# Cluster attention and a softplus FFN on one core: the first batch prepared in pairs of heads, evictions on a choice of engines, weights paced by the scores, and filler matmuls in planned waits

## The chip, the cores and the metric

The kernel runs on one core of one Trainium2 chip. The core has five engines that work side by side, each in its own program order: TensorE (PE in the profile, its weight loads PEld), VectorE (DVE), ScalarE (ACT), GpSimd (POOL) and SyncE (SP, which here only starts transfers). The metric is the device time of one execution in microseconds. The median of three runs before the change is 906.73 us.

## What is computed

Four batches of eight heads, 768 tokens, head size 64. Each query and each key is given to the nearest of 16 centroids of its head (by cosine), and a query attends only to keys of its own cluster. What comes out is a matrix of 3072 tokens by 512, which goes through a two-layer network with a softplus between the layers.

```python
q_assign = np.argmax(np.einsum('bhsd,hcd->bhsc', q_n, c_n), axis=-1)
k_assign = np.argmax(np.einsum('bhsd,hcd->bhsc', k_n, c_n), axis=-1)
mask = q_assign[:, :, :, None] == k_assign[:, :, None, :]
scores = np.where(mask, scale * np.matmul(q, k.transpose(0, 1, 3, 2)), -1000000000.0)
attn = np.exp(scores - np.max(scores, axis=-1, keepdims=True))
attn = attn / (np.sum(attn, axis=-1, keepdims=True) + 1e-09)
x = merge_heads(np.matmul(attn, v))
...
h = x @ w_in
g = np.maximum(h, 0.0) + np.log1p(np.exp(-np.abs(h)))
return (g @ w_out).astype(np.float32)
```

## The kernel before

**Numbers in two halves.** Operands of TensorE are split into a high half of 16 bits and the rest (a cast on ScalarE, then a subtraction on GpSimd); products are sums of three matmuls of halves. The mask rides along in the same matmul: the key operand carries in 16 extra columns a large negative number for every cluster that isn't its own, the query operand carries a one for its cluster, so masked scores are driven down without a separate step.

**Passes and tiles.** A pass is one batch and half of its tokens (three blocks of 128): eight passes. In a pass each of the eight heads has three score tiles of 128 queries by 768 keys, 24 tiles in all. A tile goes through `scores` (four matmuls at L544 into one of two PSUM buffers of the tag s, a row maximum on VectorE at L560, an exponential on ScalarE at L568), then the probabilities are split (L607, L609) and turned by a transposing DMA (a flip, L618), and `attend` multiplies them with the values. In pass 0 alone the probabilities stay in 32 bits, are turned on TensorE (L585), evicted from PSUM (L591 on VectorE, L593 on ScalarE) and multiplied with the raw values (L647).

**Preparation.** `prep_k` takes the keys of two heads: cast, subtract, turn (`turn`, on TensorE for batch 0 with evictions at L380 and L382, by a flip later), similarities with the centroids (`nearest`, L394 and L395), the nearest cluster, the mask (L444), a second turn. `clusters` counts by a matmul with ones (L456) which clusters have keys at all (L461, L464). `prep_q` does the like for four heads at once; it waits for the keys of all four, since queries whose cluster has no key are treated differently. `prep_v` splits the values.

**Weights.** Both weight matrices come as 64-bit floats in 32 steps of 512 columns. `prep_weights` makes 32-bit floats of their bits with one ScalarE and three VectorE instructions (L303, L305, L309, L315), then splits them (L318, L319). The raw words lie in the room of `wo` that is filled last.

**FFN.** `ffn1` of a pass starts when all four head pairs of the pass are turned into `xT` (16 blocks of twelve matmuls, L720 to L722), `softplus` works on VectorE and ScalarE (L739 to L751, split at L762 and L763), `ffn2` makes the output (L784 to L786) with two rounds of half the inner width, and `store` scales it, adds (L800, L804) and sends it (L807).

**The order.** Nothing of the order is written out by hand. Every chain of work is a Python generator that yields operations with an engine, a duration and a way to emit them. The class `Order` keeps a clock for each engine and always emits the operation that could start first by its own durations, the smaller priority number first among equals. Waits inside it (`od.set`, `wait`, rings of buffers) exist in the plan only; on the chip each engine runs its instructions in the emitted order and waits for data alone. So a changed duration, priority or planned wait changes the order of instructions on each engine, and nothing else. Transfers are planned by one clock `od.dma` for loads and flips together. VectorE and GpSimd operations marked `shared` are planned one after the other. Loads are started from ScalarE's queue (L204), flips and stores from SP's.

Of the kernel before, what the change touches and what calls it, by code (L numbers as in the profile page):

```python
# [8 lines left out]
F16 = mybir.dt.float16  # L9
# [10 lines left out]
DDS = 1024  # L20
LAG = 4
AHEAD = 10
NPE = 8
# [4 lines left out]
class Order:  # L28
# [8 lines left out]
    def __init__(self):  # L37
        self.free = dict.fromkeys(self.LAT, 0.0)
        self.ev, self.blocked, self.active = {}, {}, []
        self.dma = 0.0  # L40
        self.shared = {"DVE": 0.0, "POOL": 0.0}
        self.rings = {}
        self.cur, self.seq = None, 0

# [6 lines left out]
    def get(self, tag, size):  # L51

        k = self.rings.get(tag, 0)
        self.rings[tag] = k + 1
        return ("wait", (tag, k - size)) if k >= size else None, (tag, k)
# [23 lines left out]

    def run(self):  # L80
        while self.active:
            best = None
            for ch in self.active:
                _, eng, ns, _, opt = ch["op"]
                start = max(ch["now"], self.free[eng])
                if opt.get("shared"):
                    start = max(start, self.shared["POOL" if eng == "DVE" else "DVE"])
                prio = ch["prio"]() if callable(ch["prio"]) else ch["prio"]
                key = (start, prio, ch["seq"])
                if best is None or key < best[0]:  # L90
                    best = key, ch
            (start, _, _), ch = best
# [3 lines left out]
            if opt.get("shared"):  # L96
# [12 lines left out]
def tile_cluster_attention__then__softplus_ffn(  # L109
# [18 lines left out]
    SH = S // 2  # L128
    QT = 3

    passes = [(b, c0) for b in range(B) for c0 in range(0, NT, QT)]
    NF = DFF // P
    SCALE = 1.0 / math.sqrt(D)
    nb = QT * P

# [54 lines left out]

    def op(eng, ns, emit, **opt):
# [10 lines left out]

    def load(dst, src, nbytes):
        return op("ACT", 60, lambda: nc.scalar.dma_start(dst, src), dma=nbytes / 290.0)  # L204
# [10 lines left out]
    def prep_centroids():  # L215
# [8 lines left out]
        yield op("DVE", 150, lambda: V.tensor_tensor(sq, cf, cf, ALU.mult), dma=0)  # L224
# [45 lines left out]
    def prep_weights(step: int):  # L270
# [32 lines left out]
        yield op("ACT", 630, lambda: nc.scalar.activation(mag, val, AF.Abs, scale=sc))  # L303
# [14 lines left out]
        yield op("ACT", 610, lambda: nc.scalar.copy(part[:, 0], val))  # L318
        yield op("POOL", 1160, lambda: nc.gpsimd.tensor_tensor(part[:, 1], val, part[:, 0], ALU.subtract), shared=True)  # L319
# [11 lines left out]
    def raw_tile(nm, n, shape):  # L331

        if n < H and nm != "q":
# [3 lines left out]
        return key, p2.tile(shape, F32, tag="raw", name=f"raw{nm}_{n}")  # L337

    raw_v = {}

    def prep_v(n: int):
# [10 lines left out]
        yield op(  # L352
            "POOL",
            1640,
            lambda: nc.gpsimd.tensor_tensor(vb[:, :, :, :D], vf, vb[:, :, :, D : 2 * D], ALU.subtract),
            shared=True,
        )
# [7 lines left out]
    def turn(dst, src, name: str, on_chip: bool):  # L365
# [4 lines left out]
        for g in range(0, dst.shape[1], NT):  # L370
            hk = yield from ring("h", 2)
            ps = ps_h.tile([P, NT, P], F16, tag="h", name=f"{name}_{g}")

            def emit(g=g, ps=ps):
                for c in range(NT):
# [3 lines left out]
            if g:  # L379
                yield op("DVE", 950, lambda g=g, ps=ps: nc.vector.tensor_copy(dst[:, g : g + NT], ps))  # L380
            else:
                yield op("ACT", 820, lambda g=g, ps=ps: nc.scalar.copy(dst[:, g : g + NT], ps))  # L382
            od.set(hk)

    def nearest(xs, heads, low: int, sfx: str):
# [3 lines left out]
        ps = ps_h.tile([P, 2 * nt, NCL], F32, tag="h", name=f"sim_{sfx}")  # L389
        sim = ps[:, :nt]  # L390
# [7 lines left out]
        mx = p2.tile([P, nt, 1], F32, tag="mx", name=f"mx_{sfx}")  # L398
# [3 lines left out]
        best = p2.tile([P, nt, 1], F32, tag="best", name=f"best_{sfx}")  # L402
        yield op("DVE", 345, lambda: nc.vector.tensor_reduce(best, sim, AX.X, ALU.max))
        return ps, sim, best.to_broadcast(shp)

    def next_n2():
        key = yield from ring("n2", 2)
        return key, N2[key[1] % 2]
# [3 lines left out]
    def prep_k(n: int):  # L412
# [5 lines left out]
        nk = yield from ring("n1", 2)  # L418
        kt = p2.tile([P, 2, 2, NT, P], F16, tag="kt", name=f"kt_{n}", bufs=NP)
        kT[n], kT[n + 1] = kt[:, :, 0], kt[:, :, 1]  # L420
        n1 = p2.tile([P, 2 * NT, P], F16, tag="n1", name=f"kn1_{n}")
        od.set(("kn", n))
        yield op("ACT", 830, lambda: nc.scalar.copy(n1[:, :, D:], kf))
        yield op(
            "POOL", 1640, lambda: nc.gpsimd.tensor_tensor(n1[:, :, :D], kf, n1[:, :, D:], ALU.subtract), shared=True
        )
        od.set(rk)
        kt0 = kt[:, 0].rearrange("p h c t -> p (h c) t")
        yield from turn(kt0, n1, f"kT0_{n}", n < NPE)
        n2k, n2 = yield from next_n2()  # L430
        yield op("ACT", 830, lambda: nc.scalar.copy(n2[:, :, :D], n1[:, :, D:]))
        od.set(nk)
        h = n % H
        yield wait("cents")
        hk = yield from ring("h", 2)
        ps, sim, best = yield from nearest(
            [kt0[:, c] for c in range(2 * NT)], [h] * NT + [h + 1] * NT, 2, f"k{n}"
        )
        eq = p2.tile([P, 2 * NT, NCL], F16, tag="eq", name=f"eq_k{n}")
        yield op("DVE", 345, lambda: nc.vector.tensor_tensor(eq, sim, best, ALU.is_equal))  # L440
        yield op(
            "DVE",
            250,
# [438 lines left out]
```

## Time and profile before

| what | value |
|---|---|
| median of three runs | 906.73 us (905.98 to 908.38) |
| the profiled execution | 904.0 us, of it 902.2 us from the first to the last instruction (span) |
| mean granted clock of TensorE | 0.973 |
| busy of TensorE | 823.7 us, 91% of the span |
| busy of VectorE, ScalarE, GpSimd | 560.8, 589.4, 523.9 us |
| moved by DMA | 136 MB, 99 MB of it by flips |

The profile shows one execution. A view by stages gives the busy time of each engine in a stretch, the clock that TensorE was granted (1.00 is full speed) and the share of the 16 DMA engines that was busy. A view of waits gives, for an engine, what ended its idle time: "PE h L720 <- DVE fg L751: 6.2, 4, 3.3" says that TensorE's matmuls at line 720 waited four times for a VectorE instruction at line 751 that reads or writes fg, 6.2 us in all and 3.3 at most. In rows of instructions "x3" stands for several of one kind in a row, and the time in brackets is the idle time just before. In rows of groups the busy time and the mean duration in ns stand behind the bar.

### The profile page before, as it was taken

The page shows a single profiled execution, that of the slowest core. Times are in us where ns is not written, and L with a number is a line of the kernel's source. Part 1 is how long each engine was busy: PE and PEld are TensorE (multiplying, and loading weights), DVE is VectorE, ACT ScalarE, POOL GpSimd, SP SyncE. Part 2 cuts the span into 40 slices and gives each one's busy share as a digit, 9 for nine tenths or more (in the row PEclk, how much of TensorE's full clock was granted, in tenths as well). Part 3 has the DMA queues.
Part 4 walks back from the last instruction along what each step waited for, and adds up shares of the span by engine and source line. Part 5 has one row for each costly group of instructions (what it writes and reads, how often), then busy time and mean ns, then how long its engine had stood idle before and what let it go on. Part 6 is the DMA issues. An engine that isn't in the chain of part 4 may idle for free.

```text
span 902.2 us, 19238 instructions
## 1 busy us (share of the span) xinstructions
PE 823.7 (91%) x7843; PEld 520.0 (58%) x7843; DVE 560.8 (62%) x1034; ACT 589.4 (65%) x904; POOL 523.9 (58%) x353
## 2 busy tenths in 40 slices
PE   2669797889679999999999999999999999999996
PEld 2558684555335666666666666666666666655542
DVE  5889787778685665675766666666665645433331
ACT  5657477886458877876767777867677676633320
POOL 5233326896548778777677676776676565512210
PEclk9979699999799999999999999999999999999998
DMA  6323439999546979999888779998867755600000
GB/s 222 95 94 120 130 128 195 199 226 237 141 123 159 202 171 202 223 203 230 157 199 179 162 149 206 207 211 182 171 155 161 133 115 138 126 9 25 12 1 35
DMA packets 393320, 136.02 MB, mean 151 GB/s; under 512 B 369680, under 2 KB 386064, under 8 KB 393232
## 3 DMA queue, kind: packets, MB, share of 16 engines
q1 hardware_dynamic: 371472, 99.15, 54.9%
q10 hardware_dynamic: 21760, 35.66, 13.0%
q8 instruction: 61, 1.00, 0.5%
q14 instruction: 27, 0.22, 0.1%
HBM read 35.68 MB, written 6.29 MB: 47 GB/s over the span
## 4 chain that ended last, share of the span: by engine, by line
PE 72%; DMA 4%; DVE 3%; POOL 3%; issue 2%; ACT 2%; POOLq 0%; DVEq 0%; ACTq 0%
PE s L544 10%; PE o L786 9%; PE o L784 9%; PE o L785 9%; PE h L720 8%; PE h L722 8%; PE h L721 8%; PE av L651 3%; PE av L653 3%; PE av L652 3%; DMA pt<-phl 3%; POOL phl L609 2%; DMA xT<-xn 1%; ACT p L568 1%; DVE negm L560 1%
## 5 line engine op out<-in xcount | busy, mean ns | idle before, releaser
L609 POOL TENSOR_TENSOR phl<-p,phl 128x768 f16<-128x768 f32 x168 | 277.2, 1666 | 90.9 <-ACT phl L607 54.2
L560 DVE TENSOR_REDUCE negm<-s 128x1 f32<-128x768 f32 x192 | 182.9, 954 | 67.5 <-PE s L544 65.2
L568 ACT ACTIVATE p<-s,negm 128x768 f32<-128x768 f32 x192 | 172.3, 898 | 72.9 <-DVE negm L560 47.7
L763 POOL TENSOR_TENSOR gh<-fg,gh 128x768 f16<-128x768 f32 x64 | 105.7, 1652 | 134.5 <-ACT gh L762 134.0
L720 PE MATMUL h<-xT,wi 128*128 128x384 f16 x512 | 167.9, 328 | 14.6 <-DVE fg L751 6.2
L722 PE MATMUL h<-xT,wi 128*128 128x384 f16 x512 | 168.1, 328 | 0.0
L721 PE MATMUL h<-xT,wi 128*128 128x384 f16 x512 | 168.0, 328 | 0.0
L544 PE MATMUL s<-kt,qt 128*128 128x384 f16 x768 | 158.5, 330 | 10.2 <-ACT p L568 10.0
L784 PE MATMUL o<-wo,gh 128*128 128x512 f16 x384 | 146.3, 381 | 4.9 <-ACT gh L762 3.3
L786 PE MATMUL o<-wo,gh 128*128 128x512 f16 x384 | 146.5, 382 | 1.4 <-POOL gh L763 1.4
L785 PE MATMUL o<-wo,gh 128*128 128x512 f16 x384 | 146.4, 381 | 0.1
L741 ACT ACTIVATE fa<-fa 128x384 f32<-128x384 f32 x128 | 66.6, 521 | 114.8 <-DVE fa L739 114.1
L607 ACT CAST phl<-p 128x768 f16<-128x768 f32 x168 | 134.1, 827 | 7.1 <-DMA pt<-phl 5.5
L739 DVE TENSOR_SCALAR fa<-h 128x384 int32<-128x384 int32 x128 | 71.1, 556 | 104.0 <-PE h L722 102.8
L651 PE MATMUL av<-vb,pt 128*128 128x65 f16 x1008 | 108.7, 192 | 1.9 <-DMA pt<-phl 1.8
L652 PE MATMUL av<-vb,pt 128*128 128x64 f16 x1008 | 108.7, 192 | 0.0
L653 PE MATMUL av<-vb,pt 128*128 128x65 f16 x1008 | 108.4, 194 | 0.0
L544 PEld LDWEIGHTS <-qt 128*128 128x128 f16 x768 | 72.7, 99 | 58.5 <-issue 15.1
L751 DVE SCALAR_TENSOR_TENSOR fg<-h,fa 128x384 f32<-128x384 f32 x128 | 70.6, 552 | 57.1 <-ACT fa L742 54.5
L651 PEld LDWEIGHTS <-pt 128*128 128x128 f16 x1008 | 93.6, 98 | 15.7 <-DMA pt<-phl 3.4
L652 PEld LDWEIGHTS <-pt 128*128 128x128 f16 x1008 | 92.9, 97 | 11.8
L653 PEld LDWEIGHTS <-pt 128*128 128x128 f16 x1008 | 93.1, 97 | 0.0
(114 smaller groups left out, 1193.6 us busy)
## 6 DMA issues: line engine op xcount, KB each, us to landing
wo<-in_moe_w_in_dram ACTq DMA_DIRECT2D x16, 512.0 KB, 3.6
wo<-in_moe_w_out_dram ACTq DMA_DIRECT2D x14, 512.0 KB, 3.9
rawk<-in_k_dram ACTq DMA_DIRECT2D x16, 384.0 KB, 4.8
rawv<-in_v_dram ACTq DMA_DIRECT2D x16, 384.0 KB, 4.8
rawq<-in_q_dram ACTq DMA_DIRECT2D x16, 384.0 KB, 4.2
out_dram<-ot SPq DMA_DIRECT2D x24, 256.0 KB, 2.5
pt<-phl SPq DMA_TRANSPOSE x84, 5.5
wraw<-in_moe_w_out_dram ACTq DMA_DIRECT2D x2, 512.0 KB, 3.7
```

What stands on the lines that cost most here:

```text
L544: nc.tensor.matmul(st[:, j, :SH], qt[:, s, i], kt[:, s, NT // 2 * j : NT // 2 * (j + 1)], start=(s == 0), stop=(s == 1),)
L560: yield op("DVE", 950, lambda: nc.vector.tensor_reduce(negm, st[:, :, :SH], AX.XY, ALU.max, negate=True))
L609: "POOL", 1640, lambda: nc.gpsimd.tensor_tensor(phl[:, u, 1], p32, phl[:, u, 0], ALU.subtract), shared=True
L651: nc.tensor.matmul(av, pt[:, 0, c], vb[:, c, D : 2 * D + 1], start=(c == 0), stop=False)
L652: nc.tensor.matmul(av[:, :D], pt[:, 0, c], vb[:, c, :D], start=False, stop=False)
L653: nc.tensor.matmul(av, pt[:, 1, c], vb[:, c, D : 2 * D + 1], start=False, stop=(c == NT - 1))
L720: nc.tensor.matmul(hp, w[0], x[0], start=(c == 0), stop=False)
L721: nc.tensor.matmul(hp, w[0], x[1], start=False, stop=False)
L722: nc.tensor.matmul(hp, w[1], x[0], start=False, stop=(c == NP - 1))
L784: nc.tensor.matmul(po, g[0], wo[:, f, 0, 0], start=(f == f0), stop=False)
L785: nc.tensor.matmul(po, g[0], wo[:, f, 0, 1], start=False, stop=False)
L786: nc.tensor.matmul(po, g[1], wo[:, f, 0, 0], start=False, stop=(f == f0 + NF // 2 - 1))
```

## The change

**Preparation of the first batch.** In pass 0 the queries of a head pair are prepared by themselves (`first_q`, then `prep_q` for two heads); they wait for the living clusters of their own pair, and only where these are used. For batch 0 the keys' two operands share one tile, so the copy at L431 is dropped there, and that tile comes from buffers that are free at that time (tags xT and phl); its zero columns are cleared by four memsets on GpSimd. PSUM buffers for this preparation come from any of the tags h, o and s that has room (`bank`); those of the probabilities in pass 0 from h or o.

**Masks and clusters.** The mask is computed from the 32-bit similarities in PSUM, no longer from a 16-bit copy in SBUF; the count runs on the mask, and the living clusters come from a comparison of its sums in PSUM (two VectorE instructions as before). This holds for all batches.

**A choice of engines.** Evictions of on-chip turns and the high halves of weights go to ScalarE or VectorE, subtractions to GpSimd or VectorE, whichever the planner finds free first; a subtraction goes to VectorE only where GpSimd would end more than 2 us later, the weights' cast likewise.

**Weights.** A step of `prep_weights` waits in the plan, ahead of its first ScalarE instruction, until a given score tile has been emitted (`WGATE + step * WPACE`, step 31 at tile 43), and has a priority that goes with it.

**Planner.** Loads and flips are planned by two clocks, each at half speed while the other is at work; a flip is planned at 148 ns a block and 1200 ns behind it instead of 180 and 1500. `warm` puts matmuls of 120 columns into waits of TensorE that the plan shows to be over 600 ns, for 65% of their length. The products of pass 0 share a PSUM bank with the columns that these matmuls write.

**Others.** The last head pair of pass 0 is turned into `xT` on TensorE instead of by a flip. `ffn2` waits in the plan for its first input before it takes its PSUM buffer. Some planned durations are set anew.

The constants FIRST = 3 and MIX leave the passes and the 32-bit tiles of pass 0 as they were.

```diff
+WGATE = 0
+WPACE = 1.4
+WDUE = 4
...
+WARM = 120
+WARM_FROM = 600
+WARM_SHARE = 0.65
+SLACK = 0
+BIAS = 2000
+WBIAS = 2000
+MIX = "ffffffffffff"
+EARLY = "hos"
+PTB = "ho"
...
             self.active.remove(ch)
-            _, eng, ns, emit, opt = ch["op"]
+            if eng == "PE" and self.warm:
+                self.warm(start - self.free["PE"])
...
-            if "dma" in opt:
-                self.dma = max(self.dma, start + 900) + opt["dma"]
-                end = max(self.dma, start + ns) + 1500
+            if "flip" in opt:
+                self.flips = max(self.flips, start + 900) + opt["flip"] * (2.0 if self.loads > start else 1.0)
+                end = max(self.flips, start + ns) + 1200
+            if "load" in opt:
+                self.loads = max(self.loads, start + 1200) + opt["load"] * (2.0 if self.flips > start else 1.0)
+                end = self.loads + 1200
...
+    mbank = ps_m.tile([P, 512], F32, name="mbank")
+    idle = mbank[:, 512 - WARM :]
+
+    def warm(gap):
+        if gap > WARM_FROM:
+            for _ in range(int(gap * WARM_SHARE / 52)):
+                nc.tensor.matmul(idle, eye, ones[:, :WARM], start=True, stop=True)
...
+    def evict(dst, src, size):
+        return op(
+            ("ACT", "DVE"),
+            (180 + size * 0.8, 160 + size * 1.04),
+            (lambda: nc.scalar.copy(dst, src), lambda: nc.vector.tensor_copy(dst, src)),
+        )
+
+    def sub(dst, a, b, size):
+        return op(
+            ("POOL", "DVE"),
+            (150 + size * 1.95, 120 + size * 1.08),
+            [lambda e=e: e.tensor_tensor(dst, a, b, ALU.subtract) for e in (nc.gpsimd, nc.vector)],
+            shared=True,
+            bias=BIAS,
+        )
+
+    banks = {"s": (ps_s, 2), "h": (ps_h, 2), "o": (ps_o, 1)}
+
+    def bank(tags, shape, dtype, name):
+        tag = next((t for t in tags if od.room(t, banks[t][1])), tags[0])
+        key = yield from ring(tag, banks[tag][1])
+        return key, banks[tag][0].tile(shape, dtype, tag=tag, name=name)
...
-            "SP", 150 * blocks + 100, lambda: nc.sync.dma_start_transpose(out=dst, in_=src), dma=180.0 * blocks
+            "SP", 150 * blocks + 100, lambda: nc.sync.dma_start_transpose(out=dst, in_=src), flip=148.0 * blocks
...
-        yield op("ACT", 630, lambda: nc.scalar.activation(mag, val, AF.Abs, scale=sc))
+        gate = int(WGATE + step * WPACE)
+        if gate >= 0:
+            yield wait("sc", gate)
+        yield op("ACT", 660, lambda: nc.scalar.activation(mag, val, AF.Abs, scale=sc))
...
+        if n < H:
+            tag = "xT" if n < H // 2 else "phl"
+            keys = [(yield from ring(tag, 2))]
+            n12 = p2.tile([P, 2 * NT, P + D], F16, tag=tag, name=f"kn12_{n}")
+            n1, n2 = n12[:, :, :P], n12[:, :, D:]
+            nc.gpsimd.memset(n2[:, :, D + NCL :], 0.0)
...
-        yield op("DVE", 345, lambda: nc.vector.tensor_tensor(eq, sim, best, ALU.is_equal))
-        yield op(
-            "DVE",
-            250,
-            lambda: nc.vector.tensor_scalar(n2[:, :, D : D + NCL], eq, 1.0, MASK, ALU.subtract, ALU.mult),
-            shared=True,
-        )
+        yield op("DVE", 345, lambda: nc.vector.tensor_tensor(sim, sim, best, ALU.is_equal))
+        mask = n2[:, :, D : D + NCL]
+        yield op("DVE", 345, lambda: nc.vector.tensor_scalar(mask, sim, 1.0, MASK, ALU.subtract, ALU.mult))
...
+    def first_q(n: int):
+        qkey[n, 0] = yield from ring("qt", 2)
+        nt = passes[0][2]
+        rk, qf = yield from load_q(n, 0)
+        qt = p2.tile([P, 2, 4, nt, P], F16, tag="qt", name=f"qt_{n}_0")
+        for u in range(4):
+            qT[n + u, 0] = qt[:, :, u]
+        for u in (0, 2):
+            od.spawn(prep_q(n + u, 0, 2, qf[:, u : u + 2], qt[:, :, u : u + 2], rk if u else None), od.cur["prio"] + u * nt)
...
-        yield wait("q", n - n % 4, pi)
+        yield wait("q", n - n % (4 if pi else 2), pi)
...
-        yield flip(
-            xT[pi][:, pr].rearrange("p s c t -> p (s c) t"), t_.rearrange("p s c d -> p (s c d)"), 2 * QT
+        yield from turn(
+            xT[pi][:, pr].rearrange("p s c t -> p (s c) t"),
+            t_.rearrange("p s c d -> p (s c) d"),
+            f"xT_{pr}_{pi}",
+            pi == 0 and pr == NP - 1,
         )
...
-        od.spawn(prep_weights(step), begin - 12 + step * 0.6)
+        od.spawn(prep_weights(step), WGATE + WDUE + step * WPACE)
```

More of the change, by code (lines that the diff above doesn't have):

```diff
@@ L78, in pump, with start @@
         self.cur = outer
+    def start(self, ch, eng):
+        t = max(ch["now"], self.free[eng])
+        if ch["op"][4].get("shared") and eng in self.shared:
+            t = max(t, self.shared["POOL" if eng == "DVE" else "DVE"])
+        return t
     def run(self):
         while self.active:
-            best = None
+            ready = []
             for ch in self.active:
[L84 to L87, printed above, removed]
+                eng, ns = ch["op"][1:3]
+                if isinstance(eng, tuple):
+                    _, ns, eng = min((self.start(ch, e) + n + (e != eng[0]) * ch["op"][4].get("bias", 0), n, e) for e, n in zip(eng, ns))
@@ L88, in run @@
                 prio = ch["prio"]() if callable(ch["prio"]) else ch["prio"]
[L89 to L92, printed above, removed]
-            self.active.remove(ch)
-            _, eng, ns, emit, opt = ch["op"]
+                ready.append((self.start(ch, eng), prio, ch["seq"], eng, ns, ch))
+            soon = min(ready, key=lambda r: r[:3])
+            start, _, _, eng, ns, ch = min(
+                (r for r in ready if r[3] == soon[3] and r[0] <= soon[0] + SLACK), key=lambda r: (r[1], r[0], r[2])
+            )
@@ L337, in raw_tile, with next_n2 @@
         return key, p2.tile(shape, F32, tag="raw", name=f"raw{nm}_{n}")
+    def next_n2():
+        key = yield from ring("n2", 2)
+        return key, N2[key[2] % 2]
     raw_v = {}
@@ L447, in prep_k @@
-        od.spawn(clusters(n, ps, eq, hk), od.cur["prio"])
-        yield from turn(kt[:, 1].rearrange("p h c t -> p (h c) t"), n2, f"kT1_{n}", n < NPE)
-        od.set(n2k)
+        hk, ps = yield from bank(EARLY if n < H else "h", [P, 4 * NT, NCL], F32, f"sim_k{n}")
+        sim, best = yield from nearest(
+            ps[:, : 2 * NT], [kt0[:, c] for c in range(2 * NT)], [h] * NT + [h + 1] * NT, 2, f"k{n}"
+        )
+        yield op("DVE", 345, lambda: nc.vector.tensor_tensor(sim, sim, best, ALU.is_equal))
@@ L450, in prep_k, with clusters @@
+        mask = n2[:, :, D : D + NCL]
+        yield op("DVE", 345, lambda: nc.vector.tensor_scalar(mask, sim, 1.0, MASK, ALU.subtract, ALU.mult))
+        od.spawn(clusters(n, ps, mask, hk), od.cur["prio"])
+        yield from turn(kt[:, 1].rearrange("p h c t -> p (h c) t"), n2, f"kT1_{n}", n < H)
+        for key in keys:
+            od.set(key)
         od.set(("k", n))
-    def clusters(n, ps, eq, hk):
+    def clusters(n, ps, mask, hk):
         h = n % H
         cnt = ps[:, 2 * NT :]
-        yield op("PE", 100, lambda: nc.tensor.matmul(cnt, ones, eq, start=True, stop=True))
+        yield op("PE", 100, lambda: nc.tensor.matmul(cnt, ones, mask, start=True, stop=True))
@@ L630, in attend @@
         n, pi, i = tiles[t]
+        nt = passes[pi][2]
         h = n % H
```

289 lines of the change are left out of this document (154 added, 135 removed).

## The prediction

> **What bounds the kernel now.** I read the time by stages first, then TensorE's waits in each stage, then the order of time in the first one. The first view is the busy time of each engine by stage: the length, then busy us of PE, PEld, DVE, ACT and POOL, then the granted clock and the share of the DMA engines. The stages are the preparation before the first scores, the 24 score tiles of pass 0, the change to the mixed flow, the mixed flow itself, and the tail.
>
> ```profile
> core 0: us, PE busy (x) PEld busy (x) DVE busy (x) ACT busy (x) POOL busy (x), PEclk, DMA share, GB/s
> 0.00:54.00 54.00, 23.02 (x295) 19.48 (x296) 38.63 (x114) 28.60 (x41) 22.64 (x23) 0.92 0.46 152
> 54.00:139.00 85.00, 76.01 (x570) 64.23 (x568) 74.96 (x120) 57.26 (x113) 25.88 (x22) 0.89 0.42 121
> 139.00:300.00 161.00, 132.05 (x1329) 79.79 (x1327) 113.06 (x198) 113.63 (x173) 113.28 (x76) 0.96 0.85 185
> 300.00:860.00 560.00, 559.89 (x5508) 341.71 (x5507) 325.37 (x589) 382.23 (x566) 357.21 (x231) 1.00 0.75 155
> 860.00:902.20 42.20, 32.77 (x150) 14.81 (x148) 8.81 (x15) 7.72 (x13) 4.91 (x3) 0.92 0.05 19
> ```
>
> From 300 to 860 us TensorE is busy for 559.89 of 560 us at full clock. Its matmuls there are the same after the change, so nothing can be won in that stretch. All that can be won lies in the idle time of TensorE elsewhere: 31.0 us in the first stage, 9.0 in the second, 29.0 in the third, 9.4 in the tail, and in the granted clock, which is below 1.00 in those four alone. VectorE is busy for 75.0 of 85 us in the second stage, nearly as full as TensorE.
>
> The second view is TensorE's waits over the whole run, longest first in total (total us, times, longest).
>
> ```profile
> PE centsT L250 <- DVE cb L242: 11.3, 1, 11.3
> PE s L544 <- ACT p L568: 10.0, 10, 1.8
> PE qT L376 <- POOL n L516: 6.2, 2, 5.2
> PE h L720 <- DVE fg L751: 6.2, 4, 3.3
> PE h L720 <- DVE aq L511: 5.4, 1, 5.4
> PE sim_k L456 <- DVE eq_k L440: 3.9, 2, 3.7
> PE o L784 <- ACT gh L762: 3.3, 1, 3.3
> PE h L720 <- DMA xT<-xn: 2.9, 1, 2.9
> ```
>
> Those for centsT, qT and sim_k lie in the first stage, that of o in the tail, the others nearly all in the third stage.
>
> In the first stage TensorE waits for the elementwise engines, which prepare all eight heads before the first score. The order of time there shows the pieces that I use (start, us, engine and line):
>
> ```profile
> 16.44 0.36 DVE L399 TENSOR_REDUCE mx_k<-sim_k 128x12 f32<-128x192 f32 x1 [2.59 <-PE sim_k L395]
> ...
> 19.03 3.12 POOL L355 TENSOR_TENSOR vb<-rawv,vb 128x768 f16<-128x768 f32 x2
> 19.15 1.53 DVE L444 TENSOR_SCALAR n<-eq_k 128x192 f16<-128x192 f16 x1
> ...
> 23.69 0.20 DVE L444 TENSOR_SCALAR n<-eq_k 128x192 f16<-128x192 f16 x1
> ...
> 54.03 2.27 PE L544 MATMUL s<-kt,qt 128*128 128x384 f16 x8
> ```
>
> The similarities of the first key pair are done at 16.4 us, yet the first score starts at 54.0. L444 takes 0.20 us at one time, and 1.53 at another, when POOL starts an instruction of 3.12/2 = 1.56 just before it: some VectorE instructions stand still while POOL works.
>
> **Term 1, the first two stages.** The change lets heads 0 and 1 go ahead alone: their queries no longer wait for the keys of heads 2 and 3. I call S the start of the first score and T the time from there to the last score of pass 0.
>
> S, from the rows: similarities of the first keys ready at 16.4; five VectorE steps of 0.36 give 18.2; the mask, now read from PSUM and priced like the steps at 0.36, 18.6; the count on TensorE about 0.3 and two steps for the living clusters, 19.5; two steps for the queries, at their longest again 0.36 each, 20.2; POOL's product for half of the 768 columns that take 1.56, about 0.8, 21.0; two half transposes and their evictions some 1.5, 22.5. That is the lower bound. POOL has subtractions of about 1.56 queued ahead and the first evictions share ACT and DVE with the other heads, so one or two such instructions lie between: I take S = 26. The upper bound is 34, when five of the steps wait for a POOL instruction each (five times 1.56 on 26).
>
> T. What is moved behind the first score must now run beside the tiles. The rows give L315, one of three VectorE instructions of a weight step, by stage (us and count), then the other two, L309 and L305, over the whole run (us, then mean ns), then the evictions of the scores' transposes on both engines:
>
> ```profile
> 0.00:54.00 54.00, 2.74 (x4) 0.92 0.46 152
> 54.00:139.00 85.00, 14.81 (x17) 0.89 0.42 121
> 139.00:300.00 161.00, 10.39 (x11) 0.96 0.85 185
> ...
> L309 DVE SCALAR_TENSOR_TENSOR wo<-wo 128x512 int32<-128x512 int32 x14 | 11.2, 800 | 0.4
> L305 DVE TENSOR_SCALAR wo<-wo 128x512 int32<-128x512 int32 x16 | 10.7, 671 | 0.8 <-ACT wo L303 0.8
> ...
> L591 DVE COPY ptf<-pT 128x384 f32<-128x384 f32 x24 | 13.2, 550 | 3.3 <-PE pT L585 3.2
> ...
> L593 ACT COPY ptf<-pT 128x384 f32<-128x384 f32 x24 | 11.5, 478 | 7.4 <-PE pT L585 5.3 <-issue 2.1
> ```
>
> A weight step costs VectorE 14.81/17 + 0.80 + 0.67 = 2.34 us. Of the first stage's 38.6 us some 10 are weights (four steps and begun ones) and some 7 the centroids and memsets, which leaves 21 for keys and queries; three quarters of it, 15 to 16, move behind S. Weights: step s may begin with score 1.4 s, so steps 0 to 17, 18 of them, fall due within pass 0, where 17 ran in the second stage, one more. So VectorE has 75.0 + 15.5 + 2.3 = 92.8 us. ScalarE had 57.3; of the first stage's 28.6 some 17 remain when the table load, the weights and the four copies L431 (dropped) are taken off, three quarters of it make 70, and one more weight step some 71. The evictions go to either engine, at 0.55 us on VectorE against 0.48 on ScalarE, so 8 to 9 us can pass over: 84 and 79. TensorE had 76.0; three quarters of the first stage's 23.0 would add 17 at the speed that they had there, half as much at full clock: I take 10, as the transposes mostly run beside dense work. A slow clock goes off again if the waits are filled:
>
> ```profile
> 96.00:116.00 20.00, 16.77 (x103) 14.17 (x102) 13.99 (x26) 8.81 (x18) 6.96 (x6) 0.57 0.38 109
> ```
>
> 16.77 us at a clock of 0.57 lose 16.77 x 0.43 = 7.2. TensorE then needs 79, or 86 if the clock falls as before. So T is bound by VectorE at 84 or TensorE at 86, whichever is worse. The second stage ran at 75.0/85 = 88% of VectorE; at that share T = 95, at 95% 88. I take 94. S + T = 120 against 139, a gain of 19. The bounds are 22.5 + 87 = 110 (a gain of 29) and 34 + 105 = 139 (none), the latter with no eviction passed over (92.8 at 88%).
>
> **Term 2, the last pair's transposes on chip.** FFN 1 of pass 0 waited 2.9 us for the flip of xT. Six transposes, at the first stage's 23.0/295 = 0.08 us an instruction 0.5 us, and two evictions of some 0.5 take its place. I take 2 of the 2.9; bounds 0 and 2.9.
>
> **Term 3, the third stage.** 14 weight steps remain instead of 11. At 2.34 us each that is 7 us more of VectorE, which is 113 of 161 us full; it has 48 us of cover, and without it all 7 show. I put 2 against the change. For it stand subtractions that may go to VectorE where POOL would end over 2 us later (POOL is 113 of 161 full), and filled waits: I put 3. The moved weights' loads leave ScalarE's queue later, too; each takes a slot in it and no wait of TensorE. Sum +1; bounds -7 and +14 (half of the 29 us idle).
>
> A VectorE subtraction isn't shown before. The nearest row is L485, two SBUF operands of 768 columns:
>
> ```profile
> L485 DVE SCALAR_TENSOR_TENSOR qn<-rawq,qn 128x768 f16<-128x768 f32 x16 | 16.4, 1023 | 2.9 <-ACT qn L481 2.9
> ```
>
> It costs 1.02 us, or 1.02 + 1.56 behind a POOL instruction, in place of 1.56 on POOL. [...]
>
> **Term 4, the tail and the filler.** After its wait of 3.3 us the last FFN 2 starts at a low clock:
>
> ```profile
> 883.09 0.61 PE L786 MATMUL o<-wo,gh 128*128 128x512 f16 x1 [0.94 <-POOL gh L763]
> ...
> 893.22 0.38 PE L784 MATMUL o<-wo,gh 128*128 128x512 f16 x1 [0.78 <-DVE ot L804]
> ```
>
> The planner fills 65% of a planned wait with matmuls of 120 columns. They read two constants and write columns that nothing uses, so they wait for nothing; what stands behind them on TensorE is the next real matmul. If the wait is real they are free, and here they save the slow start: 42.2 us at 0.92 lose 0.08 x 32.8 = 2.6, I take 2. If a planned wait isn't there they delay TensorE by their own length, at most 0.65 of all idle time of before, 0.65 x 78.5 = 51 us; I take nothing, as the planner's waits before the steady stretch stand in for real ones. [...]
>
> **Sum.** 19 + 2 + 1 + 2 = 24. The profiled execution took 904.0 us (span 902.2, 1.8 around it): 880.0. The median of the runs shown is 906.7, 2.7 above it, so I forecast **882**. Its own range is 868 to 896.
>
> **Rivals.**
> *More than that* (866): S = 24, T = 89, and term 3 gives 10: 26 + 2 + 10 + 2 = 40. For it: of the 29 us idle in the third stage 11.6 wait for VectorE (fg and aq). Against: weights are added there.
> *Given back* (902): the first scores come early, but the scores of the next batch start no sooner, as the flips keep the DMA engines 0.85 busy in the third stage, or S = 30 and T = 102 with the added weights at full price: 7 + 2 - 7 + 2 = 4.
> *It doesn't come early*: TensorE runs in the planned order, and one late link (centroids at 11.3 us) holds the rest; S stays above 45, and terms 2 to 4 are left: about 902.
> *Slower* (916): the planner now gives a flip 148 ns a block and 1.2 us instead of 180 and 1.5, so for 24 blocks it places the product behind it 24 x 0.032 + 0.3 = 1.07 us sooner.
>
> ```profile
> pt<-phl SPq DMA_TRANSPOSE x84, 5.5
> ...
> PE av L651 <- DMA pt<-phl: 1.8, 2, 1.3
> ```
>
> There are 84 such flips, landing 5.5 us after issue, and a mean wait of 24/84 = 0.29 us for each would eat the gain; at 0.4 us it is 34 us, 10 slower than before. Against: TensorE waited for them only twice, 1.8 us in all, as products stand four tiles behind.
>
> **How the numbers follow.** Forecast 0.53, more 0.16, given back 0.16, not early 0.04, slower 0.11. A measurement of this kernel can tell about 0.3%, 2.7 us, from no change; 902 lies a little beyond it, so of the 0.20 at 902 I count 0.12 as faster and 0.07 as the same. Faster 0.81, same 0.07, slower 0.12. The range from 857 to 905 leaves out the slower case and the edges of two others, 0.19 in all; the bounds of terms 1 and 3 reach beyond it only together.
>
> **What would show it.** Right: the first L544 (in its new line) near 26 us, the last score of pass 0 near 120, VectorE over 88% between, TensorE full from about 280 on, no wait for xT before the first FFN 1, the last FFN 2 at 0.38 us throughout. Wrong: a first score after 34 us (term 1), a stretch without scores in the third stage longer than before (given back), waits of av for pt in the steady stretch (slower), or filler matmuls there, which would mean that the planner sees waits that the chip doesn't have.

## The result: slower, and the profile after

The changed kernel takes 914.22 us (median of 17 runs) where the kernel before takes 906.33 in 17 runs beside it: a ratio of 1.008, 95% interval 1.0061 to 1.01. The forecast was 882 and the range 857 to 905, so it failed on the side as well as on the size. The profiled execution is the longest of the 17: 921.48 us, 919.3 of it span, so its rows overstate the loss by some 7 us.

The view by stages of the changed kernel, in the stretches used before (length, then busy us of PE, PEld, DVE, ACT and POOL, the granted clock, the share of the DMA engines):

```profile
core 0: us, PE busy (x) PEld busy (x) DVE busy (x) ACT busy (x) POOL busy (x), PEclk, DMA share, GB/s
0.00:54.00 54.00, 44.07 (x593) 39.32 (x594) 39.60 (x133) 36.13 (x64) 23.14 (x27) 0.94 0.49 159
54.00:139.00 85.00, 77.52 (x728) 67.98 (x727) 68.93 (x121) 59.23 (x112) 33.24 (x27) 0.92 0.51 125
139.00:300.00 161.00, 138.61 (x1688) 96.00 (x1686) 118.43 (x201) 109.27 (x168) 110.10 (x73) 0.98 0.99 186
300.00:860.00 560.00, 549.72 (x5373) 332.74 (x5372) 316.93 (x567) 371.02 (x552) 353.44 (x229) 1.00 0.80 153
860.00:919.30 59.30, 54.22 (x341) 29.26 (x339) 15.25 (x27) 14.61 (x25) 9.05 (x6) 0.99 0.05 19
```

Two things are to be seen. TensorE is busier in the first three stages, though partly with filler. And the steady stretch, which was full, now leaves TensorE idle for 560 - 549.72 = 10.3 us, with the DMA engines 0.80 busy instead of 0.75. The waits of TensorE over the whole run say on what:

```profile
PE mbank L758 <- DMA pt<-phl: 15.4, 9, 3.9
PE h L836 <- DVE fg L868: 7.9, 7, 2.0
PE s L655 <- ACT p L679: 7.5, 9, 1.8
```

L758 is the first of the three matmuls of a product (L651 before; mbank is its PSUM tile now). It waits nine times for the flip of the probabilities, 15.4 us, where it waited twice, 1.8 us. The first score came early all the same. In this view of one line's instructions the three durations are ns (shortest, median, longest), then come the first and the last start:

```profile
L655 PE MATMUL s<-kt,qt x768: 322/326/527, 29.4 to 799.6; 128*128 128x384 f16 x192
```

**A ledger of useful work.** To see where an early start is lost, I counted in each profile the matmuls of scores, FFN 1, FFN 2, products and turned probabilities that lie before a time, each at its length at full clock. They are counted in slices of 20 us and scaled to the number that both kernels execute, since a matmul across the border of two slices is counted in both; the leads are good to 1 or 2 us. The difference to the profile before, in us of TensorE's work, is the lead. It holds no fillers. All kernels of the table are described below.

| at (us) | changed | old, phl 128 bytes on | changed, phl at 256 | at 512 | at 512, no fillers | at 512, weights cut |
|---|---|---|---|---|---|---|
| 60 | +19.0 | -1.0 | +20.0 | +19.9 | +16.5 | +19.6 |
| 120 | +18.4 | -3.7 | +21.6 | +21.7 | +20.4 | +21.8 |
| 140 | +8.0 | -4.7 | +12.2 | +12.3 | +8.6 | +12.9 |
| 220 | +1.0 | -6.6 | +12.1 | +12.4 | +8.0 | +13.4 |
| 300 | -7.0 | -6.0 | +8.5 | +10.8 | +1.3 | +15.1 |
| 500 | -11.4 | -12.3 | +8.6 | +9.7 | +2.6 | +15.8 |
| 860 | -19.4 | -14.4 | +5.2 | +9.8 | +1.3 | +12.1 |

The changed kernel is 18.4 us ahead at 120 us, as term 1 had it. By 300 us it has lost 25.4, and between 300 and 860 another 12.4.

### The profile page after: what moved, and what is told of

Same layout as the page of the kernel before. It is cut to its first block, busy times and chain, and to the rows that moved or that the text cites. A ratio compares the mean times of both kernels' runs of the same rounds, so it can differ in the third digit from the quotient of the medians.

```text
span 919.3 us, 21027 instructions
## 1 busy us (share of the span) xinstructions
PE 864.1 (94%) x8715; PEld 565.3 (61%) x8715; DVE 559.1 (61%) x1046; ACT 590.3 (64%) x918; POOL 529.0 (58%) x359
## 2 busy tenths in 40 slices
DMA packets 392527, 135.94 MB, mean 148 GB/s; under 512 B 368880, under 2 KB 385264, under 8 KB 392432
## 3 DMA queue, kind: packets, MB, share of 16 engines
q1 hardware_dynamic: 370672, 98.95, 60.5%
q10 hardware_dynamic: 21760, 35.66, 12.9%
## 4 chain that ended last, share of the span: by engine, by line
PE 55%; DMA 10%; ACT 2%; DVE 2%; issue 2%; POOL 1%; POOLq 0%; SPq 0%; DVEq 0%; ACTq 0%
DMA pt<-phl 9%; PE s L655 7%; PE o L904 7%; PE o L902 7%; PE o L903 7%; PE h L836 6%; PE h L838 6%; PE h L837 6%; PE mbank L758 2%; PE mbank L760 2%; PE mbank L759 2%; POOL phl L259 1%; DMA wo<-in_moe_w_out_dram 1%; ACT p L679 1%; ACT phl L715 0%
## 5 line engine op out<-in xcount | busy, mean ns | idle before, releaser
L758 PE MATMUL mbank<-vb,pt 128*128 128x65 f16 x1008 | 109.4, 193 | 15.7 <-DMA pt<-phl 15.4
L758 PEld LDWEIGHTS <-pt 128*128 128x128 f16 x1008 | 93.9, 99 | 31.4 <-DMA pt<-phl 21.0
L759 PE MATMUL mbank<-vb,pt 128*128 128x64 f16 x1008 | 109.3, 193 | 0.0
L760 PE MATMUL mbank<-vb,pt 128*128 128x65 f16 x1008 | 109.0, 195 | 0.0
```

The lines of the kernel that those rows point to most:

```text
L758: nc.tensor.matmul(av, pt[:, 0, c], vb[:, c, D : 2 * D + 1], start=(c == 0), stop=False)
L759: nc.tensor.matmul(av[:, :D], pt[:, 0, c], vb[:, c, :D], start=False, stop=False)
L760: nc.tensor.matmul(av, pt[:, 1, c], vb[:, c, D : 2 * D + 1], start=False, stop=(c == NT - 1))
```

## The experiments

### Parts of the change undone

My first theory was that the fillers delay TensorE. The view of groups has all of them in one row:

```profile
L230 PE MATMUL mbank<-ones,eye 128*128 128x120 f16 x866 | 57.7, 225 | 5.9 <-DVE x L792 4.0 <-DVE ones L203 1.8
```

866 matmuls, 57.7 us of busy time. Rivals were the flips planned too soon (the slower rival of the prediction), the weights held back, and the choice of engines.

**No fillers.** Edit: `-    od.warm = warm`.

> The changed kernel without its filler matmuls; the planned order is untouched. In the changed kernel 866 fillers keep TensorE busy for 57.7 us. Theory A (the fillers delay real work, since planned waits and real waits don't coincide): the fillers before the first scores are free (16 us), those in the tail too (5 us), most of the rest, some 35 us, is paid in part: faster than the changed kernel by 12 to 25 us, about 895. Theory B (they only fill real waits, and the loss comes from the order): within 4 us of the changed kernel or a little slower for the lost clock, 912 to 918.

Measured: 923.39 us, ratio 1.0152 (1.0123 to 1.0181), mean clock 0.965 instead of 0.983. The theory fell: the fillers save some 0.7%, they don't cost.

**Flips planned as before**, at 180 ns a block and 1500 behind it, the two clocks kept; with and without fillers.

```diff
-                end = max(self.flips, start + ns) + 1200
+                end = max(self.flips, start + ns) + 1500
...
-            "SP", 150 * blocks + 100, lambda: nc.sync.dma_start_transpose(out=dst, in_=src), flip=148.0 * blocks
+            "SP", 150 * blocks + 100, lambda: nc.sync.dma_start_transpose(out=dst, in_=src), flip=180.0 * blocks
```

> The changed kernel with a flip planned at 180 ns a block and 1500 ns behind it, as before the change. Theory F (products placed too soon wait for their flips): waits of the products for pt fall from 15.4 us to under 4, and the time by about 10 us, to 904. Theory A (fillers): waits fall or not, the time stays within 4 us of 914, as fillers are still there.

> Both at once: no fillers, and flips planned as before the change. If fillers and flips are separate losses they add: about 885 to 890. If one stands for the other, no better than the better of the two alone.

Measured: 932.57 (1.0294, 1.027 to 1.0318) and 931.98 (1.0285, 1.026 to 1.031). TensorE's waits for pt fall from 15.4 us to 8.8, without fillers from 23.9 to 5.1, and yet later flips in the plan make it worse, not better. With two clocks, each at half speed beside the other, and the longer flips, the plan sees waits that aren't there: 234 fillers fall between 300 and 860 us, where the changed kernel has none.

**Weights not held until the first scores**; **transfers planned on one clock at the old figures**; **no choice of engines** for subtractions and the weights' casts (the evictions keep theirs).

```diff
-WGATE = 0
+WGATE = -999
...
-        od.spawn(prep_weights(step), WGATE + WDUE + step * WPACE)
+        od.spawn(prep_weights(step), H * QT + AHEAD - 12 + step * 0.6)
```

> The changed kernel with the weights planned as before (no wait for a score, the old priorities). Theory W (the held weights crowd VectorE and POOL from 140 to 300 us): the first scores come some us later, but the stretch from 140 to 300 us shrinks and the time falls by 8 us or more. Theories A and F: the time stays or grows, 912 to 925.

```diff
-                self.flips = max(self.flips, start + 900) + opt["flip"] * (2.0 if self.loads > start else 1.0)
-                end = max(self.flips, start + ns) + 1200
+                self.flips = max(self.flips, start + 900) + opt["flip"]
+                end = max(self.flips, start + ns) + 1500
...
-                self.loads = max(self.loads, start + 1200) + opt["load"] * (2.0 if self.flips > start else 1.0)
-                end = self.loads + 1200
+                self.flips = max(self.flips, start + 900) + opt["load"]
+                end = max(self.flips, start + ns) + 1500
...
+            "SP", 150 * blocks + 100, lambda: nc.sync.dma_start_transpose(out=dst, in_=src), flip=180.0 * blocks
```

> The changed kernel with the transfers planned as before the change: one clock for loads and flips, 180 ns a block, 1500 ns behind. All else of the change stays. Theory P (the two planned clocks make an order that suits the chip worse in passes 1 to 7): the lead of the front, 18 us at 120 us, is kept and the time is 890 to 895. Theory R (any change of planned durations reshuffles the order, and the order of before is a lucky one): between 905 and 935.

```diff
-BIAS = 2000
-WBIAS = 2000
+BIAS = 1000000000
+WBIAS = 1000000000
```

> The changed kernel with all subtractions on GpSimd and all weight casts on ScalarE, as before; the evictions keep their choice. Theory C (subtractions on VectorE block GpSimd and VectorE from 120 to 300 us): the lead stays above 10 us at 220 us and the time falls below 905. Theory R: between 905 and 935, with no pattern.

Measured: 929.35 (1.0261, 1.022 to 1.0302), the first score at 37.1 us, so holding the weights, with the priorities that go with it, pays; 908.59 (1.0024, 1.0 to 1.0049), some 0.6% below the changed kernel; 912.81 (1.0079, 1.0048 to 1.0111), so that choice of engines brings nothing that can be measured. None of them is faster than the kernel before.

**The old kernel with parts of the plan changed.** First the flips planned at 148 ns a block and 1200 behind it, on its one clock; then, to learn what a mere change of order does, the exponential planned at 910 ns instead of 900.

```diff
-                end = max(self.dma, start + ns) + 1500
+                end = max(self.dma, start + ns) + (1200 if eng == "SP" else 1500)
...
-            "SP", 150 * blocks + 100, lambda: nc.sync.dma_start_transpose(out=dst, in_=src), dma=180.0 * blocks
+            "SP", 150 * blocks + 100, lambda: nc.sync.dma_start_transpose(out=dst, in_=src), dma=148.0 * blocks
```

> The kernel before with one thing of the change: a flip planned at 148 ns a block and 1200 ns behind it. The slower rival of the prediction: products wait for flips, 84 times 0.3 to 0.4 us, 925 to 940. Theory R: between 900 and 930; waits for pt need not grow.

```diff
-        yield op("ACT", 900, lambda: nc.scalar.activation(p32, st[:, :, :SH], AF.Exp, bias=negm, **tot))
+        yield op("ACT", 910, lambda: nc.scalar.activation(p32, st[:, :, :SH], AF.Exp, bias=negm, **tot))
```

> The kernel before with one planned duration moved by 1%: the exponential at 910 instead of 900 ns (the profile has it at 898). No instruction is added or dropped. If the plan is steady: within 3 us of before, 904 to 909. Theory R: 6 us or more away, on either side, more likely slower, to 920.

Measured: 915.89 (1.0125, 1.0088 to 1.0163) and 912.36 (1.0059, 1.0033 to 1.0086). The first of them shows the mechanism of my slower rival, in the waits of TensorE:

```profile
PE av L651 <- DMA pt<-phl: 11.4, 11, 3.5
```

11.4 us in 11 waits, with flips no slower than before (median 3093 ns): products really were placed too soon. But the second shows that an edit of 1% in one planned duration, with no meaning of its own, is worth 0.6%: single edits of the plan of that size or less, the 0.6% of the one clock among them, say little.

### Where the buffers lie

In the changed kernel the flips pt<-phl held SP's queue longer, at the median 3.67 us instead of 3.09. In the view of the flips' instructions from 300 to 800 us (ns: shortest, median, longest), first before, then after:

```profile
engine op xcount: duration ns min/median/max, first and last start us, forms
...
L209 SPq DMA_TRANSPOSE pt<-phl x67: 2892/3092/6740, 301.4 to 785.1; - x67
```

```profile
L278 SPq DMA_TRANSPOSE pt<-phl x65: 3435/3674/5377, 305.4 to 796.4; - x65
```

Even the shortest takes 0.54 us more, so it isn't only queueing. What the flip moves is the same. The list of queues on the two pages, before and after (packets, MB, share of 16 engines):

```profile
q1 hardware_dynamic: 371472, 99.15, 54.9%
```

```profile
q1 hardware_dynamic: 370672, 98.95, 60.5%
```

What differs is the place. The pool hands out addresses in the order in which tags are first used. The change takes the keys' shared tiles early from the tags xT and phl, drops the tag eq and doubles two small ones, and so moves nearly every buffer: phl from 210688 to 181120 bytes (256 and 384 beyond a multiple of 512), pt from 182976 to 207040 (192 beyond, both). So I fixed the order of the tags by reserving them ahead of all else, instructions unchanged:

```diff
+    for tag, n, size in (("x32", 1, 1536), ("g", 8, 3072), ("kt", 4, 6144), ..., ("phl", 2, 6144), ("fg", 2, 3072)):
+        for _ in range(n):
+            p2.tile([P, size], mybir.dt.uint8, tag=tag, name=f"at_{tag}", bufs=n)
```

The changed kernel at the old places, the old kernel at the new places, the old kernel with 128 unused bytes ahead of phl (so that only phl and fg move), and the changed kernel at the old places with transfers planned on one clock:

> The changed kernel, instruction for instruction, with its SBUF buffers at the addresses that the kernel before gives them. In every run so far the transfer pt<-phl holds SP's queue for 3.1 us (median) in kernels with the places of before and for 3.7 us in kernels with the places of the change. Theory L (the places make these flips slower, and 84 slower flips cost the passes 1 to 7): 3.1 us again, landing at 4.7 instead of 5.5, waits of the products for pt under 6 us instead of 15, the time 900 to 906. Theory R (only the order counts): 3.7 us or not, the time stays at 911 to 917.

> The mirror image: the kernel before, instruction for instruction, with its buffers at the addresses of the changed kernel (the upper ones 512 bytes on). Theory L: pt<-phl at 3.7 us, products that wait for pt, 912 to 920. Theory R: 904 to 909.

> The kernel before with phl and fg moved up by 128 bytes and nothing else. Before, phl starts at 256 beyond a multiple of 512, in the changed kernel at 384. Theory L by alignment of the source: 3.7 us for pt<-phl and 912 to 920. Theory L by distance or other tiles: 3.1 us and 904 to 909.

> The changed kernel with the places of before and with the transfers planned by one clock as before (e5, which came to 908.6). Theory L: another 5 to 10 us less than e5, 897 to 903, faster than both kernels, since the front's lead of 18 us is lost in part only. Theory R: 905 to 915.

| kernel | time | ratio to before (interval) | median flip in SP's queue, 300 to 800 us |
|---|---|---|---|
| changed, old places | 896.15 | 0.9911 (0.988 to 0.9942) | 3113 ns |
| old, new places | 914.62 | 1.0114 (1.0083 to 1.0146) | 3700 |
| old, phl 128 bytes on | 913.73 | 1.0108 (1.0073 to 1.0144) | 3729 |
| changed, old places, one clock | 896.96 | 0.9907 (0.9883 to 0.9932) | – |

This turns the result round. At the old places the change makes the kernel faster by 0.9%; at the new places the old kernel is slower by 1.1%, and 128 bytes ahead of phl do all of that:

```profile
L236 SPq DMA_TRANSPOSE pt<-phl x69: 3419/3729/6127, 296.3 to 799.6; - x69
```

TensorE's waits for these flips go with it: in the changed kernel they fall from 15.4 us to 4.2 at the old places, in the old kernel 128 bytes raise them from 1.8 to 7.8. Both rows are of the whole run:

```profile
PE mbank L784 <- DMA pt<-phl: 4.2, 5, 1.3
```

```profile
PE av L678 <- DMA pt<-phl: 7.8, 9, 2.2
```

One clock instead of two was worth 0.6% at the new places (1.0024 against 1.008), no more than the nudge above, and nothing at the old ones (0.9907 against 0.9911).

### The start of phl alone

The changed kernel, with paddings only: 384 bytes ahead of phl and 128 behind (phl at 181504, 256 beyond a multiple of 512), the same exchanged (181248, a multiple of 512), the first with the target pt at 256 too, and the first with the sources of the other flips (kn, qn) at 256 too.

```diff
+        ("pa", 1, 384),
+        ("phl", 2, 6144),
+        ("pb", 1, 128),
```

> The changed kernel, instruction for instruction, with two unused paddings only: 384 bytes ahead of phl, 128 behind it. phl then starts 256 bytes beyond a multiple of 512 (181504, after 181120, which is 384 beyond), what follows moves by 512, and all else stays where the change put it. Theory (the start of the flip's source within 512 bytes sets its time): the flips pt<-phl hold SP's queue for a median of 3.1 us as before instead of 3.7, and the time is that of the kernel at the old places, 894 to 900, ratio to before 0.988 to 0.993. Rival (which buffers are neighbours, or the whole set of addresses, counts): 3.7 us and 910 to 916.

> The same with the paddings exchanged: 128 bytes ahead of phl, 384 behind it, so phl starts at a multiple of 512 (181248). If a multiple of 256 is what counts, 3.1 us a flip and 894 to 900. If the place 256 beyond a multiple of 512 has its own worth, between 3.1 and 3.7 us or above, 900 to 916. If a multiple of 512 is better still, below 3.0 us and 890 to 896.

> As the first of this group, and the flips' target pt moved by 64 bytes too, from 192 to 256 beyond a multiple of 512 (207616). If only the source counts: the time of the first within 0.3%. If the target's start counts as the source's does: below 3.0 us a flip and 4 to 10 us off the time. The target was 192 beyond in every kernel so far, so neither is shown yet; I expect the first, with the flips at 3.1 us.

> As the first of this group, and the sources of the flips of keys and queries (kn, qn) also 256 beyond a multiple of 512 instead of 384: the 384 bytes stand ahead of them. If the rule holds for every flip: the flips kt<-kn and qt<-qn hold the queue for some 15% less, the scores of a later batch wait less for them, and the time is 0 to 4 us below the first of this group. If the rule holds for phl alone: the same time within 0.3%.

| phl, other | time | ratio to before (interval) |
|---|---|---|
| at 256 | 896.4 | 0.9918 (0.9893 to 0.9944) |
| at 512 | 894.23 | 0.9888 (0.9867 to 0.9909) |
| at 256, pt at 256 | 897.06 | 0.9913 (0.9898 to 0.9929) |
| at 256, kn and qn at 256 | 894.67 | 0.9886 (0.9868 to 0.9905) |

The flips of these four in the same view, one fence for each kernel in the same order; of the third and the fourth also those of the queries, whose sources start at 384 and at 256:

```profile
L305 SPq DMA_TRANSPOSE pt<-phl x64: 2926/3134/6236, 302.1 to 779.3; - x64
```

```profile
L305 SPq DMA_TRANSPOSE pt<-phl x64: 3002/3123/6696, 299.5 to 775.9; - x64
```

```profile
L305 SPq DMA_TRANSPOSE pt<-phl x64: 2962/3112/5752, 303.8 to 780.4; - x64
...
L305 SPq DMA_TRANSPOSE qt<-qn x9: 1275/1506/2675, 319.2 to 692.6; - x9
```

```profile
L305 SPq DMA_TRANSPOSE pt<-phl x64: 2967/3124/6235, 300.0 to 776.5; - x64
...
L305 SPq DMA_TRANSPOSE qt<-qn x9: 1275/1477/2258, 315.6 to 688.7; - x9
```

In this view of the kernels shown here and of six more with parts of the change or of the plan altered, the median is 3.09 to 3.13 us at 256 and at 512, 3.66 to 3.78 at 384: of the places tried, those at a multiple of 256 bytes are the quick ones. Moving the target's start made no difference (3.13 us at 192 beyond, 3.11 at 256). For qn and kn nothing is seen in the queue (qn 1.48 us at 256 and 1.51 at 384, kn 1.47 and 1.51), and the times of the four don't tell apart. So the cause of the loss is shown: the pool's new order put phl 128 bytes beyond a multiple of 256, and the two paddings alone make 894 to 896 us of 914. With phl at 512 the waits for pt and the two later stages, to be set beside those of the changed kernel above, are:

```profile
PE mbank L785 <- DMA pt<-phl: 1.9, 2, 1.1
```

```profile
139.00:300.00 161.00, 147.83 (x1769) 100.93 (x1767) 118.64 (x207) 117.08 (x179) 118.93 (x79) 1.00 0.94 191
300.00:860.00 560.00, 557.91 (x5372) 336.96 (x5370) 317.25 (x570) 367.40 (x549) 344.92 (x222) 1.00 0.71 149
```

These kernels are faster than the one before and than the changed one; which of the four is the fastest can't be told.

A block of 128 x 128 in 16 bits is 256 bytes of each partition; the flips' queue carries 98.95 MB, of which 6.3 MB are the 24 stores; the rest, in the 368880 packets that the profile counts under 512 bytes, is 251 bytes a packet. In the changed kernel the flips hold SP's queue for a median of 3.67 us from 384 beyond a multiple of 512 and for 3.12 from a multiple of 512, 18% more; from 256 beyond it is 3.13, the same as from a multiple. Why those from 384 are slower is not shown.

### What is left at a good place

Two more kernels with phl at 512: without the fillers; and with two of three VectorE instructions of the weights' steps 18 to 31 left out, in an unchanged order.

```diff
-            lambda: nc.vector.scalar_tensor_tensor(high, low, 29, high, ALU.logical_shift_right, ALU.bitwise_or),
+            lambda: None if step >= 18 else nc.vector.scalar_tensor_tensor(high, low, 29, high, ALU.logical_shift_right, ALU.bitwise_or),
```

> The kernel with phl at a multiple of 512 (894 us), without the filler matmuls; nothing else differs. If the fillers are worth as much here as at the changed places (there their loss cost 9 us, at a clock of 0.965): 900 to 906, ratio to before 0.995 to 1.002, the clock 0.96 to 0.97, so that with good places nearly all of the gain left at the end is theirs. If they only covered for the late flips: within 3 us of 894.

> The kernel with phl at a multiple of 512 (894 us), the same order of all instructions that stay; of the weights' steps 18 to 31 two of the three VectorE instructions are left out (28 instructions, about 25 us of VectorE between 120 and 290 us; the weights are then not the right numbers). That kernel leads the old one by 21.7 us of TensorE's work at 120 us and by 10.8 at 300. If VectorE, full with weights in the third stage, eats this lead: the lead at 300 us stays at 16 to 22 and the time falls to 883 to 889. If it is lost to something else (flips and loads, exponentials, the order): a lead of 9 to 13 and 891 to 896.

Measured: 906.51 (0.9997, 0.9976 to 1.0018) and 892.6 (0.9848, 0.981 to 0.9885). The stretch from 120 to 300 us in the view by stages: before, phl at 512, the same without fillers, the same with the weights cut:

```profile
120.00:300.00 180.00, 150.24 (x1474) 95.38 (x1473) 130.65 (x224) 128.13 (x200) 120.03 (x81) 0.96 0.82 181
```

```profile
120.00:300.00 180.00, 164.40 (x1992) 112.91 (x1989) 136.51 (x233) 131.63 (x202) 132.05 (x88) 1.00 0.95 193
```

```profile
120.00:300.00 180.00, 144.81 (x1439) 88.59 (x1439) 139.41 (x235) 130.16 (x200) 130.70 (x87) 0.91 0.90 190
```

```profile
120.00:300.00 180.00, 167.46 (x2045) 115.06 (x2043) 118.33 (x207) 133.39 (x204) 133.93 (x90) 1.00 0.93 198
```

Without fillers the clock there is 0.91, the lead falls from 20.4 to 1.3, and the kernel takes as long as before: the early start by itself is given back whole. With fillers the clock is 1.00, and 10.8 of 21.7 are left. Taking 18.2 us of VectorE away (136.51 to 118.33) keeps 15.1: of the 10.9 us lost between 120 and 300, some 3 to 4 go with that part of the weights. By the ratios its time is 0.4% below (0.9848 against 0.9888), with intervals that overlap, so this stands on the ledger alone. Most of the rest goes at once, between 120 and 140: 9.4 us, 11.8 without fillers, 8.9 with the weights cut. There the changed kernels have already begun FFN 1 (at 127.7 us with phl at 512, at 148.6 before) and the transfers of the mixed flow, while the old one still works on pass 0. With phl at 512 VectorE is busy for 18.9 of these 20 us, the share of the DMA engines is 1.01 (0.53 before), and 4.7 us of TensorE's busy time are fillers. Whether that loss is the mixed flow's own slower pace or an order that could be mended wasn't tried.

## Why the prediction was wrong

**The length of the flips, taken over unchanged: this step failed, in the bound of the steady stretch and in term 3.** The prediction said of 300 to 860 us "Its matmuls there are the same after the change, so nothing can be won in that stretch", and took for granted that nothing can be lost there, save by products planned sooner; term 3 too has no price for a slower flip. What it left out is that a change of which tile is asked for first moves buffers. The 84 flips got slower by some 0.6 us each (medians of those from 300 to 800 us: 3.67 against 3.09); against the same kernel with phl at 512, the share of the DMA engines is 0.99 instead of 0.94 in the third stage and 0.80 instead of 0.71 in the steady one, and products wait for pt 15.4 us instead of 1.9. By the ratios that is 1.6 to 1.9% of 906, 15 to 17 us, and it alone turns a gain into a loss. In the ledger, whose profiled execution is some 7 us longer than the median, more of it falls between 120 and 300 us (25.4 lost against 10.9) than between 300 and 860 (12.4 against 1.0). The diff shows tags used earlier and one dropped, so that buffers move could be seen; that the place has a price was in no row of the kernel before.

**Term 1: right.** The first score came at 29.4 us (26 expected, 22.5 to 34 the bounds), and at 28.4 with phl at 512. The lead at 120 us is 18.4 and 21.7, where a gain of 19 was expected at that time. The last transpose of probabilities in pass 0 starts at 118.8 and 111.7 us, before at 134.6. VectorE was busy for 79.7 of the 90.6 us from 29.4 to 120 with phl at 512, 88%, as assumed; in the changed kernel's profile it was 74.8, 83%, below the 88% that were to show the term right, at a clock of 0.92.

**Term 2: right as far as it shows.** No wait for xT is left in the list of waits.

**Term 3: wrong, beyond its lower bound.** +1 expected, -7 to +14 the bounds; with quick flips 21.7 - 10.8 = 10.9 us are lost between 120 and 300, and 19.1 without fillers. I gave the three weight steps that move into that stage 2 us; in the cut kernel two of three VectorE instructions of all 14 steps are worth some 3 to 4, so the weights aren't the bulk. Subtractions that may go to VectorE aren't it either, as far as the changed kernel shows: without that choice it takes as long (1.0079 against 1.008). What is left is the loss that comes with the other chains of the stage when they start 20 us sooner; which of them it is stays open.

**Term 4: the fillers were undersized.** I counted 2 for the tail and, in term 3, 3 for filled waits and moved subtractions together. At the good place they are worth 0.9997 - 0.9888 = 1.1%, 9.9 us, by the clock from 120 to 300 us (1.00 instead of 0.91) more than by the tail: of the 11.1 us between the spans of the two profiles (901.8 and 890.7), some 8 are there at 860 us and some 3 come behind it. From 100 to 120 us, where the prediction had filled waits end the slow clock, it is 1.00 with fillers at the good place and 0.83 without; in the changed kernel's profile it was still 0.84 from 54 to 96 us. No filler fell into the steady stretch.

**The rivals.** *Given back* (902) describes the kernel at a good place without fillers: about the same time as before. The reason that it names, flips that keep the DMA engines busy, was not tested; their share from 120 to 300 us is 0.90 there. *Slower* (916) gave nearly the right time by a cause that isn't the main one. Sooner products do cost: the old kernel with that edit lost 1.25%, where a nudge without meaning lost 0.6%. But without slow flips the new plan costs the changed kernel nothing, and with the plan set back at the new places it is still no faster than before (1.0024), while the paddings alone bring it to 0.9888. *It doesn't come early* fell with the first score at 29.4 us, and *more* didn't come.

With the place mended the sum is 21.7 by 120 us, less 10.9 by 300, less 1.0 by 860, and 1.7 in the tail: 11.5, the difference of the two spans (902.2 and 890.7). So without the buffers' places the side would have been right, and the forecast of 882 still 12 too low, in the main by term 3.

## What to carry to other kernels

A change that uses a tile earlier or drops one can move every buffer behind it, so a comparison of two kernels compares two layouts as well: look at the addresses of transfers' sources before reading the time, and fix the order of tags where they differ; here 128 bytes ahead of one buffer cost 1.1%. An early start can be lost in the next stage (here 10.8 of 21.7 us were left at 300 us, 1.3 of 20.4 without fillers); ask for each stage what it does with work that comes 20 us sooner. In a planned order measure what a meaningless nudge does before an edit of the plan is believed.

## What the runs showed of the hardware that was not expected

The transposing transfers of 24 blocks from SBUF to SBUF (pt<-phl) held their queue for a median of 3.1 us where the source started at a multiple of 256 bytes (two places tried) and for 3.7 us where it started 128 beyond (384 of 512; 128 of 512 wasn't tried). Moving the target's start from 192 to 256 beyond a multiple of 512 made no difference (3.13 and 3.11 us). For the flips of qn no difference was seen between 384 and 256 (1.51 and 1.48 us).

Matmuls that compute nothing, 866 of them in the changed kernel, cut the time by 0.7% at the new places and by 1.1% with phl at 512: there the mean granted clock of the profiled executions is 0.998 with them and 0.972 without.
